# Routing two sequences of a top-2 mixture of experts in one pass, with one-hot tables built on ScalarE

## The chip, the cores and the metric

One NeuronCore of one Trainium2 chip runs the kernel. The metric is the device time of one execution in microseconds (us). PE is TensorE, DVE is VectorE, ACT is ScalarE, POOL is GpSimd; SP issues most of the transfers. Sequences, chunks, blocks and experts are counted from 0.

## The reference

Four sequences of 768 tokens go through linear attention with decay, with 8 heads of width 64; the 3072 rows of width 512 then go through a mixture of 8 experts, two for each token.

```python
for t in range(S):                      # attention, each batch and head
    state = gamma * state + outer(k[t], v[t])
    y[t] = scale * q[t] @ state
x = y as rows of tokens                 # [3072, 512]
noisy = x @ w_gate + log1p(exp(x @ w_noise)) * noise
top2, weights = the two largest of noisy, softmax over the two
out[token] += weight * (relu(x[token] @ w1[e]) @ w2[e])   # for both experts e of a token
```

## The kernel before

**The chunk loop.** The tokens are worked in 24 chunks of 128, six to a sequence, by a loop over j whose order is written out by hand. Iteration j gives PE, in this order: `qk(j+1)` (scores of the next chunk, into two PSUM buffers `pA`), `x_turn(j-1)` (attention rows turned to token rows, with the router's logits and the sums of squares, into `pT`, of which there is one), `y_state(j)` (not in a sequence's first chunk), what stands in the list `middle`, then `y_mm(j)` (output into `pY`, and the state update except in a sequence's last chunk). DVE masks the scores (`am`, two products of 128x512), reduces the logits, makes the row scale, and writes the low half of `x_split` after ACT has written the high half; a store to `xbuf` in DRAM follows on SP's queue. ACT empties `pY` (`yt`), the state (`U`) and squares (`sq`). POOL multiplies queries and values by decay tables (`q_scale`, `v_scale`). SP's queue issues the loads of chunk j+4.

Between these stand small steps put in place by iteration: the list `mid` is issued ahead of `x_split(j-1)`, `todo` behind it, `first_todo` (`at0`) behind `sq(j)`. They are the routing of each finished sequence, the half parts of expert 0's weights (`w_lo_half`, 16 instructions of 128x512 on DVE), and the zeroing of the output (`zero_out`, SP).

**Routing.** For each sequence b: `route_x` (softplus, ACT), `route_b` (noisy logits), `route_t` and `route_i` (max and index, one instruction pair for each chunk), `route_m` (one-hots of the two experts), `route_p` (counts on PE), `route_n`, `route_g`, `route_d` (gates, positions), `rest_a`, `rest_r` (slot numbers of the other experts). `own_a` to `own_t` then build, for expert 0, a 128x768 one-hot `a0` of each token's lane and a table `bb0`; `own_m` multiplies them on PE into the slot list of expert 0, `slots` turns it into row numbers. Sequences 0 and 1 fill the first three blocks of expert 0 (384 slots), whose rows are fetched by an indirect DMA on POOL's queue (`gather`) and turned by a DMA transpose on SP's queue (`x_t`). In the loop the three gathers stand in iterations 19, 20, 20 and the transposes in 20, 21, 21.

**Behind the loop.** `early(n)` issues n units of expert 0's first 384 columns: eight `mm1` units (12 matmuls of 384 columns, then `hh` on ACT and `hl` on DVE), three `mm2` blocks. The first unit stands ahead of `x_turn` of chunk 23. Between units come the routing of sequence 3, its own tables, `rest_b` for each sequence, and `rest(n)`: for each of 8 pairs (sequence, choice) two one-hots and a table on DVE (`rest_c`, `rest_d`) and six matmuls (`rest_e`), which give the slots of experts 1 to 7. Experts 1 to 7 follow, each with its gathers, `mm1` columns and `mm2` blocks; a loop for overfull experts ends the kernel.

Of the kernel before, what the change touches and what calls it, by code (L numbers as in the profile page):

```python
# [20 lines left out]
C = 128  # L21
# [76 lines left out]
def moe_kernel(ctx, tc, qT, kT, kt, vt, noise, wgn, w1, w2, ctab, qtab, xbuf, out):  # L98
# [236 lines left out]
    def y_mm(j):  # L335
# [15 lines left out]
        SQ[j] = loads.tile([128, KT, C], BF, name="sq", bufs=2)  # L351
        nc.scalar.activation(SQ[j].rearrange("p n c -> p (n c)"), y, AF.Square)

    def x_turn(j):
# [12 lines left out]
        if c == 0:  # L367
            LG[b] = work.tile([128, NC, 2 * E], F32, name="lg")
# [56 lines left out]
    def route_m(b):

        ny, m8, i8 = R[b]
        oh = work.tile([128, 2, NC, NL], F32, name="oh")
        s4 = [128, 2, NC, NL]
        nc.vector.tensor_tensor(oh, K("lidx")[:, None, None, :].to_broadcast(s4),  # L430
                                i8[:, :, 0:2].rearrange("p c k -> p k c")[:, :, :, None].to_broadcast(s4), op=OP.is_equal)
# [4 lines left out]
        R[b] = (oh, mb, den)
        R["mb", b] = mb

    def route_c(b):

        oh, mb, den = R[b]
        nc.scalar.activation(den, den, AF.Exp)

    def route_p(b):
        mb = R.pop(("mb", b))
        nc.tensor.matmul(POS[:, :NC, :], trib, mb, start=True, stop=True, skip_group_check=True)
        for c in range(NC):
            n = NC - c
            nc.tensor.matmul(POS[:, c + 1:, :], oneb, mb[:, c:c + 1, :].to_broadcast([128, n, NL]),
                             start=False, stop=True, skip_group_check=True)  # L450
# [708 lines left out]
```

## Time and profile before

| | |
|---|---|
| median of 3 runs | 680.64 us (679.03 to 682.36) |
| profiled execution | 680.02 us, span 678.2 us |
| granted clock of TensorE, mean | 0.989 |
| busy over the span | PE 96%, DVE 46%, ACT 43%, POOL 30% |
| chain that ended last | PE 73%, DVE 10%, DMA 7%, issue 6% |

The span runs from the first to the last instruction of the core; the rest of the execution's time lies around it. Shares over the whole span hide the stages: the chunk loop lasts until about 124 us, the experts from there on. A busy PE is not PE at its peak, since matmuls are pipelined; a granted clock of 1.00 is 2.4 GHz, 0.50 is 1.2 GHz.

### The profile page before, as it was taken

The numbers are of one execution on the slowest core, as the hardware profiler recorded it, in microseconds if no ns is written. First come the engines' busy times: TensorE is split into PE (matmuls) and PEld (weight loads), VectorE is DVE, ScalarE is ACT, GpSimd is POOL, SyncE is SP. The second block draws the span as 40 slices with busy tenths as digits, with TensorE's granted clock in tenths as the row PEclk, the third lists the DMA queues.
The fourth block names the chain that finished last, engine by engine and source line by source line (L and its number), as shares of the span: only waits on it lengthen the run. The fifth ranks groups of instructions, "written<-read, shape, count | busy, mean of one in ns | idle before, by whom it ended". The sixth has DMA issues, their size and how long they took to land.

```text
span 678.2 us, 13086 instructions
## 1 busy us (share of the span) xinstructions
PE 648.3 (96%) x5325; PEld 404.5 (60%) x5325; DVE 308.9 (46%) x790; ACT 294.5 (43%) x521; POOL 200.3 (30%) x158
## 2 busy tenths in 40 slices
PE   7998989999999999999999999999999999999991
PEld 5987878657768745554555455545554565456440
DVE  4699999699877321532053205320622162225100
ACT  4785544412645533543354335434543454434110
POOL 3456355033054034203420342044204410430021
PEclk9999999999999999999999999999999999999996
DMA  9999778949487747644764487547645664660132
GB/s 336 393 381 374 258 249 253 343 136 196 152 157 114 267 77 132 200 140 78 134 191 140 82 125 194 140 78 139 180 140 94 124 199 114 120 125 5 16 47 32
DMA packets 90718, 112.87 MB, mean 166 GB/s; under 512 B 57216, under 2 KB 57472, under 8 KB 87072
## 3 DMA queue, kind: packets, MB, share of 16 engines
q1 hardware_dynamic: 78736, 84.95, 41.0%
q0 software_dynamic: 11344, 26.22, 21.6%
q10 hardware_dynamic: 576, 0.84, 0.4%
q8 instruction: 43, 0.70, 0.4%
q14 instruction: 19, 0.16, 0.1%
HBM read 72.67 MB, written 26.21 MB: 146 GB/s over the span
## 4 chain that ended last, share of the span: by engine, by line
PE 73%; DVE 10%; DMA 7%; issue 6%; ACT 1%; POOL 1%; SPq 0%; POOLq 0%; ACTq 0%
PE pH L834 11%; PE pH L836 11%; PE pH L835 11%; PE pO L866 10%; PE pO L868 10%; PE pO L867 10%; DMA out<-ot,idx 4%; PE pT L365 3%; PE pA L317 2%; PE pY L339 2%; DVE am L320 2%; DVE x L390 1%; DMA xe<-xg 1%; PE pY L332 1%; DVE bb L600 1%
## 5 line engine op out<-in xcount | busy, mean ns | idle before, releaser
L855 POOL DMA_INDIRECT out<-ot,idx x54 | 89.9, 1666 | 342.1 <-ACT ot L850 209.3
L834 PE MATMUL pH<-xe,w1h 128*128 128x384 f16 (+5 forms) x576 | 180.8, 314 | 1.8 <-DMA xe<-xg 1.3
L836 PE MATMUL pH<-xe,w1l 128*128 128x384 f16 (+5 forms) x576 | 180.9, 314 | 0.0
L835 PE MATMUL pH<-xe,w1h 128*128 128x384 f16 (+5 forms) x576 | 180.8, 314 | 0.0
L838 DVE SCALAR_TENSOR_TENSOR hl<-pH,hh 128x384 f16<-128x384 f32 (+5 forms) x144 | 75.4, 527 | 190.8 <-ACT hh L837 190.6
L868 PE MATMUL pO<-w2h,hl 128*128 128x512 f16 x384 | 145.5, 379 | 0.0
L867 PE MATMUL pO<-w2l,hh 128*128 128x512 f16 x384 | 145.5, 379 | 0.0
L866 PE MATMUL pO<-w2h,hh 128*128 128x512 f16 x384 | 145.5, 379 | 0.0
L837 ACT ACTIVATE hh<-pH 128x384 f16<-128x384 f32 (+5 forms) x144 | 67.1, 467 | 134.5 <-PE pH L836 132.5
L850 ACT ACTIVATE ot<-pO,gse 128x512 f32<-128x512 f32 (+4 forms) x54 | 37.1, 687 | 171.0 <-PE pO L868 166.5
L206 DVE SCALAR_TENSOR_TENSOR w1l<-wst,wsc,w1h 128x1024 f16<-128x1024 f32 x28 | 35.8, 1284 | 105.9 <-ACT w1h L201 105.9
L713 POOL DMA_INDIRECT xg<-xbuf,idx x54 | 56.1, 1039 | 75.6 <-DVE wacc L621 30.4
L834 PEld LDWEIGHTS <-w1h 128*128 128x128 f16 x576 | 56.9, 99 | 31.3 <-issue 1.5
L836 PEld LDWEIGHTS <-w1l 128*128 128x128 f16 x576 | 56.3, 98 | 30.9
L835 PEld LDWEIGHTS <-w1h 128*128 128x128 f16 x576 | 56.3, 98 | 30.7 <-issue 0.9
L184 ACT ACTIVATE junk<-wst 128x1024 bf16<-128x1024 f32 x64 | 67.2, 1050 | 0.4 <-DMA wst<-w 0.2
L868 PEld LDWEIGHTS <-hl 128*128 128x128 f16 x384 | 37.6, 98 | 45.3
L866 PEld LDWEIGHTS <-hh 128*128 128x128 f16 x384 | 38.1, 99 | 43.9
L867 PEld LDWEIGHTS <-hh 128*128 128x128 f16 x384 | 37.5, 98 | 44.0
L297 POOL TENSOR_TENSOR qs<-in_q,gq 128x512 f32<-128x512 f32 x23 | 29.3, 1275 | 49.3 <-PE pY L332 18.2
L365 PE MATMUL pT<-turn,yt 128*128 128x144 f32 x192 | 30.6, 304 | 6.5 <-DVE x L390 4.4
L201 ACT ACTIVATE w2h<-wst,wsc 128x1024 f16<-128x1024 f32 x32 | 36.5, 1140 | 0.2 <-DVE wsc L162 0.2
(170 smaller groups left out, 684.0 us busy)
## 6 DMA issues: line engine op xcount, KB each, us to landing
wst<-w SPq DMA_DIRECT2D x28, 1024.0 KB, 7.6
in_q<-qT SPq DMA_DIRECT2D x24, 256.0 KB, 5.1
in_k<-kT SPq DMA_DIRECT2D x24, 256.0 KB, 5.2
in_v<-vt SPq DMA_DIRECT2D x24, 256.0 KB, 5.1
in_kt<-kt SPq DMA_DIRECT2D x24, 256.0 KB, 5.2
xbuf<-x SPq DMA_DIRECT2D x24, 256.0 KB, 5.1
out<-zero SPq DMA_DIRECT2D x6, 1024.0 KB, 8.4
wst<-w SPq DMA_DIRECT2D x8, 512.0 KB, 6.5
```

The costliest lines, as they stand in the source:

```text
L184: nc.scalar.activation(junk, st[:, i * 1024:(i + 1) * 1024], AF.Square, accum_out=ss[:, i:i + 1])
L365: nc.tensor.matmul(p[:, s, g * 128:g * 128 + XW], y[:, s, g, :], turn[:, v, 2 * s + g], start=(g == 0), stop=True, skip_group_check=True)
L713: nc.gpsimd.indirect_dma_start(out=x[:n], out_offset=None, in_=xbuf[:128 + B0 * S] if e == 0 and t < 3 else xbuf, in_offset=bass.IndirectO ...
L834: nc.tensor.matmul(p[:, :n], whi, xh, start=(k == 0), stop=False)
L835: nc.tensor.matmul(p[:, :n], whi, xl, start=False, stop=False)
L836: nc.tensor.matmul(p[:, :n], wlo, xh, start=False, stop=(k == KT - 1))
L837: nc.scalar.activation(hh[:, f, n0:n1], p[:, :n], AF.Relu)
L838: nc.vector.scalar_tensor_tensor(hl[:, f, n0:n1], p[:, :n], 0.0, hh[:, f, n0:n1], op0=OP.max, op1=OP.subtract)
L855: nc.gpsimd.indirect_dma_start(out=out, out_offset=bass.IndirectOffsetOnAxis(ap=idx[:n, i:i + 1], axis=0), in_=ot[:n], in_offset=None, com ...
L866: nc.tensor.matmul(p, a, WT["2h"][:, f, :], start=(f == 0), stop=False)
L867: nc.tensor.matmul(p, a, WT["2l"][:, f, :], start=False, stop=False)
L868: nc.tensor.matmul(p, c, WT["2h"][:, f, :], start=False, stop=(f == FT - 1))
```

## The change

Sequences 0 and 1 form group 0 (12 chunks), sequences 2 and 3 are groups 1 and 2; `SPAN` gives first chunk and count. The routing steps of group 0 run once over 12 chunks, except `route_x`, `route_b`, max and index, which run on six chunks each in iterations 6 to 8 and 12 to 14. `rest_a`, `rest_r` and `rest_b` leave the loop and run once over all 24 chunks behind it. The one-hots of group 0, and those of the `rest` pairs of sequences 0 and 1, are made by ACT as relu(1 - (lane - number)^2): one Square for each chunk, with the negative lane number as bias, and one Relu over six chunks. The gathers move to iterations 20, 21, 21, the transposes to 21, 22, 22. `own_a`, `own_h`, `own_b` of sequence 2 and half part 4 of w2 go behind the loop; half parts of the weights get other iterations; `sq` has one buffer. `rest_e` lags two parts instead of one. The core of the diff:

```diff
+    sfa = consts.tile([128, 2, NCH], F32, name="sfa")
+    ga = consts.tile([128, 2, NCH], F32, name="ga")
+    nla = consts.tile([128, 2, NCH], F32, name="nla")
+    lfa = consts.tile([128, 2, 2, NCH], BF, name="lfa")
...
+    POS = {n: pR[:, :(n + 1) * NL].rearrange("p (c e) -> p c e", c=n + 1) for n in (NC, 2 * NC)}
+    LST = [pR[:, 160:160 + NV * NBLK].rearrange("p (v n) -> p v n", v=NV) for g in range(1)]
     SUM = pR[:, 480:488]
+
+    SPAN = {0: (0, 2 * NC), 1: (2 * NC, NC), 2: (3 * NC, NC)}
+
+    def temp(shape, dt, name, n):
+        pool = RP[0] if n == NCH else work
+        return pool.tile(shape, dt, name=f"{name}_{n}", **({} if n == NC else dict(bufs=1)))
...
-        SQ[j] = loads.tile([128, KT, C], BF, name="sq", bufs=2)
+        SQ[j] = loads.tile([128, KT, C], BF, name="sq", bufs=1)
...
+    def route_b(g, c0, c1):
+
+        b0, n = SPAN[g]
...
+            R[g] = temp([128, n, NL], F32, "ny", n), temp([128, n, 8], F32, "m8", n), temp([128, n, 8], U32, "i8", n)
+        ny = R[g][0][:, c0:c1]
+        nc.vector.tensor_tensor(sp[:, c0:c1], sp[:, c0:c1], nz[:, b0 + c0:b0 + c1, :], op=OP.mult)
         nc.vector.memset(ny[:, :, 0:1] if o else ny[:, :, E:NL], -3.0e38)
-        nc.vector.tensor_tensor(ny[:, :, o:o + E], sp, lg[:, :, :E], op=OP.add)
-        m8 = work.tile([128, NC, 8], F32, name="m8")
-        R[b] = (ny, m8, work.tile([128, NC, 8], U32, name="i8"))
...
+    def own_a(g):
...
         nc.vector.tensor_scalar(lb[:, 1], si, 7, None, op0=OP.arith_shift_right)
-        lf = work.tile([128, 2, NC], BF, name="lf0")
+        lf = temp([128, 2, n], BF, "lf0", n)
         nc.vector.tensor_copy(lf, lb)
-        R["own", b] = lf
-
-    def own_h(b):
-        lf = R["own", b]
-        a = work.tile([128, NC, 128], BF, name="a0", bufs=2)
-        nc.vector.tensor_tensor(a, lanes[:, None, :].to_broadcast([128, NC, 128]),
-                                lf[:, 0, :, None].to_broadcast([128, NC, 128]), op=OP.is_equal)
-        R["own", b] = (lf, a)
+        if g == 0:
+            R["nl", g] = nl = temp([128, n], F32, "nl0", n)
+            nc.vector.tensor_scalar(nl, lb[:, 0], -1.0, None, op0=OP.mult)
+        R["own", g] = lf, temp([128, n, 128], BF, "a0", n)
+
+    def one_hot(a, nl):
+
+        n = nl.shape[-1]
+        for c in range(n):
+            nc.scalar.activation(a[:, c], lanes, AF.Square, bias=nl[:, c:c + 1])
+        nc.scalar.activation(a, a, AF.Relu, bias=1.0, scale=-1.0)
+
+    def own_h(g, c0, c1):
+        lf, a = R["own", g]
+        s3 = [128, c1 - c0, 128]
+        if g == 0:
+            one_hot(a[:, c0:c1], R["nl", g][:, c0:c1])
+            return
+        nc.vector.tensor_tensor(a[:, c0:c1], lanes[:, None, :].to_broadcast(s3),
+                                lf[:, 0, c0:c1, None].to_broadcast(s3), op=OP.is_equal)
 
...
+    def rest_a():
+
+        s3 = [128, NCH, NL]
+        ov = temp(s3, F32, "ov", NCH)
+        sl = temp(s3, F32, "sl", NCH)
+        nc.vector.tensor_scalar(ov, posb, float(CAP), BIG, op0=OP.is_ge, op1=OP.mult)
+        nc.vector.tensor_tensor(sl, posb, K("base")[:, None, :].to_broadcast(s3), op=OP.add)
+        nc.vector.tensor_tensor(ov, ov, sl, op=OP.add)
+        t = temp([128, 2, NCH, NL], F32, "t", NCH)
+        nc.vector.tensor_tensor(t, oh, ov[:, None].to_broadcast([128, 2, NCH, NL]), op=OP.mult)
+        nc.vector.tensor_reduce(sfa, t, axis=AX.X, op=OP.add)
+
+    def rest_b():
+
+        si = temp([128, 2, NCH], I32, "si", NCH)
+        nc.vector.tensor_copy(si, sfa)
+        lb = temp([128, 2, 2, NCH], I32, "lb", NCH)
         nc.vector.tensor_scalar(lb[:, 0], si, 127, None, op0=OP.bitwise_and)
         nc.vector.tensor_scalar(lb[:, 1], si, 7, None, op0=OP.arith_shift_right)
-        nc.vector.tensor_copy(lfa[:, b], lb)
-        gate_parts([vvb[:, b, :, :, v] for v in range(NV)], ga[:, b], [2, NC])
+        nc.vector.tensor_copy(lfa, lb)
+        nc.vector.tensor_scalar(nla, lb[:, 0], -1.0, None, op0=OP.mult)
+        gate_parts([vvb[:, :, :, v] for v in range(NV)], ga, [2, NCH])
 
...
-        nc.vector.tensor_tensor(a, lanes[:, None, :].to_broadcast([128, NC, 128]),
-                                lf[:, 0, k, :, None].to_broadcast([128, NC, 128]), op=OP.is_equal)
+        if b < B0:
+            one_hot(a, nla[:, k, b * NC:(b + 1) * NC])
+        else:
+            nc.vector.tensor_tensor(a, lanes[:, None, :].to_broadcast([128, NC, 128]),
+                                    lf[:, 0, k, :, None].to_broadcast([128, NC, 128]), op=OP.is_equal)
...
 
-    for b in range(B - 1):
-        j = (b + 1) * NC
-        r = [(f, (b,)) for f in (route_b, route_m, route_n, route_g, route_d, rest_a, rest_r, own_a, own_h, own_b, own_t)]
-        at0(j, route_x, b)
-        put_steps(j + 1, [r[0]], [(route_t, (b, 0)), (route_t, (b, 1)), (route_i, (b, 0))])
-        put_steps(j + 2, [(route_i, (b, 1))], [r[1]])
-        at0(j + 2, route_c, b)
-        middle.setdefault(j + 3, []).append((route_p, b))
-        put_steps(j + 3, [r[2]], [r[3], r[4]])
-        put_steps(j + 4, [r[5]], [r[6], r[7]])
-        put_steps(j + 5, [r[8]], [r[9]])
-        if b < B - 2:
-            put_steps(j + 6, [r[10]])
-            middle.setdefault(j + 7, []).append((own_c if b == 0 else own_m, b))
-        if b == 1:
-            put_steps(j + 7, [(own_s, (b,)), (slots, (0, 3))])
-            for t in range(3):
-                at(j + 7 + (t > 0), gather, 0, t)
-                at(j + 8 + (t > 0), x_t, 0, t)
+    mid = {}
...
+    def P(j, f, *a, d=mid):
+        d.setdefault(j, []).append((f, a))
+
+    for j, c in ((6, 0), (12, 6)):
+        at0(j, route_x, 0, c, c + 6)
+        P(j + 1, route_b, 0, c, c + 6)
+        P(j + 1, route_t, 0, c, c + 3)
+        at(j + 1, route_t, 0, c + 3, c + 6)
+        P(j + 2, route_i, 0, c, c + 3)
+        at(j + 2, route_i, 0, c + 3, c + 6)
+    P(15, route_m, 0)
+    at0(15, route_c, 0)
+    P(16, route_p, 0, d=middle)
+    P(16, route_n, 0)
+    at(16, route_g, 0)
+    P(17, route_d, 0)
+    at(17, own_a, 0)
+    at0(17, own_h, 0, 0, 6)
+    at0(18, own_h, 0, 6, 12)
+    at(18, own_b, 0)
+    at(19, own_t, 0)
+    P(20, own_m, 0, d=middle)
+    P(20, own_s, 0)
+    P(20, slots, 0, 3)
+    for t in range(3):
+        at(20 + (t > 0), gather, 0, t)
+        at(21 + (t > 0), x_t, 0, t)
+    at0(18, route_x, 1, 0, 6)
+    at(20, route_b, 1, 0, 6)
+    P(21, route_t, 1, 0, 3)
+    at(21, route_t, 1, 3, 6)
+    at(21, route_i, 1, 0, 3)
+    P(22, route_i, 1, 3, 6)
+    at(22, route_m, 1)
+    at0(22, route_c, 1)
+    P(23, route_p, 1, d=middle)
+    P(23, route_n, 1)
+    at(23, route_g, 1)
+    at(23, route_d, 1)
     at(0, turn_table, 0)
     at(3, turn_table, 1)
     for i in range(4):
...
-    for w, d in (("1", ((mid, 6), (todo, 6), (mid, 8), (todo, 8), (todo, 10), (todo, 11), (todo, 12), (todo, 14))),
-                 ("2", ((todo, 14), (todo, 16), (todo, 17), (mid, 18), (todo, 18)))):
+    for w, d in (("1", ((mid, 6), (todo, 6), (mid, 9), (todo, 9), (mid, 10), (todo, 10), (mid, 11), (todo, 11))),
+                 ("2", ((todo, 15),) + ((mid, 17), (mid, 18), (mid, 19),))):
         for i, (d, j) in enumerate(d):
             d.setdefault(j, []).append((w_lo_half, (0, w, i)))
     at(2, nc.vector.tensor_copy, lanes, K("lanes"))
...
     def rest(n):
-        while done:
+        while len(done) > (1 if n else 0):
             rest_e(*done.pop(0))
         for _ in range(n):
             if parts:
...
     x_turn(j)
-    own_t(b - 1)
     logits(j)
-    route_x(b)
...
+    route_b(2, 0, NC)
     MM[1] = True
-    for i in range(2):
-        route_t(b, i)
-    for i in range(2):
-        route_i(b, i)
-    route_m(b)
-    route_c(b)
+    route_t(2, 0, NC)
+    route_i(2, 0, NC)
+    route_m(2)
+    route_c(2)
+    own_a(1)
+    own_h(1, 0, NC)
     early(2)
-    route_p(b)
-    route_n(b)
-    own_c(b - 1)
-    route_g(b)
+    own_b(1)
+    own_t(1)
+    route_p(2)
+    route_n(2)
+    route_g(2)
     early(1)
-    route_d(b)
-    own_a(b)
-    own_h(b)
+    route_d(2)
+    own_a(2)
+    own_h(2, 0, NC)
     early(1)
-    own_b(b)
-    own_t(b)
-    w_lo_half(0, "2", 5)
+    own_c(1)
+    own_b(2)
+    own_t(2)
+    for i in [4, 5, 6, 7][:2]:
+        w_lo_half(0, "2", i)
     early(1)
-    w_lo_half(0, "2", 6)
-    w_lo_half(0, "2", 7)
+    for i in [4, 5, 6, 7][2:]:
+        w_lo_half(0, "2", i)
     early(1)
     out_scale(0, 0, 3)
 
...
     hook.append(third)
     early(1)
-    rest_a(b)
-    rest_r(b)
-    rest_b(0)
+    rest_a()
+    rest_b()
     rest(1)
+    early(1)
     ranks()
-    rest_b(1)
     for r in range(E - 1):
...
     w_load(1, "2", 0, 2)
     w_load(1, "2", 2, 2)
     out_scale(0, 3, NBLK)
-    early(1)
-    rest(2)
+    rest(1)
     early(len(units))
+    rest(1)
     for t in range(3):
...
                     w_sum(1, "12"[(n - 7) // 4], (n - 7) % 4)
                 if more and e and len(cols) * FT - 5 <= n < len(cols) * FT - 1:
                     w_sum(e + 1, "1", n - (len(cols) * FT - 5))
-                if e == 0 and n in (1, 8):
-                    rest_b(b - 1 if n == 1 else b)
-                if e == 0 and n in (0, 3, 6, 10, 13):
+                if e == 0 and n in (1, 4, 7, 10, 13):
                     rest(1)
                 n += 1
         if more and e:
...
```

## Rows read from the trace of the kernel before

**Rows 1.** Busy time in stretches of 25 us: engines, granted clock, DMA share, GB/s.
```profile
50.00:75.00 25.00, 21.81 (x333) 19.55 (x333) 24.01 (x68) 13.58 (x27) 12.47 (x11) 0.93 0.92 338
75.00:100.00 25.00, 21.64 (x353) 19.27 (x351) 23.86 (x82) 12.70 (x23) 13.34 (x12) 1.00 0.76 249
...
125.00:150.00 25.00, 24.45 (x160) 13.99 (x158) 19.29 (x92) 5.99 (x14) 3.09 (x4) 1.00 0.65 235
...
225.00:250.00 25.00, 25.00 (x147) 14.16 (x146) 6.85 (x14) 10.65 (x19) 4.54 (x4) 1.00 0.45 131
```

**Rows 2.** The same for the chunk loop: PE, weight load, DVE, ACT, POOL.
```profile
12.91:124.05 111.14, 102.30 (x1661) 91.98 (x1658) 97.98 (x331) 66.20 (x130) 53.66 (x46) 0.98 0.91 319
```

**Rows 3.** Waits of PE in the chunk loop: us in total, times, longest.
```profile
PE pT L365 <- DVE x L390: 4.4, 5, 1.5
PE pA L317 <- issue: 1.9, 2, 1.2
PE pT L365 <- DVE cb L475: 1.4, 2, 0.8
PE pT L365 <- DVE m L418: 0.7, 2, 0.5
```

**Rows 4.** Timeline of PE: qk of four iterations, first matmul of expert 0.
```profile
21.77 1.16 PE L317 MATMUL pA<-qs,in_k 64*128 64x128 f32 x16
...
26.21 1.16 PE L317 MATMUL pA<-qs,in_k 64*128 64x128 f32 x16
...
95.58 1.70 PE L317 MATMUL pA<-qs,in_k 64*128 64x128 f32 x16 [1.20 <-issue]
...
124.05 0.34 PE L834 MATMUL pH<-xe,w1h 128*128 128x384 f16 x1
```

**Rows 5.** PE busy time and granted clock in stretches of 1 us.
```profile
65.00:66.00 1.00, 0.05 (x1) 0.96 0.70 268
66.00:67.00 1.00, 1.00 (x4) 0.50 0.50 180
...
69.00:70.00 1.00, 1.00 (x24) 0.83 0.84 219
```

**Rows 6.** Timelines of DVE and POOL: masking products, route_b's product, POOL's product.
```profile
40.29 1.28 DVE L320 TENSOR_TENSOR am<-pA,ct 128x512 f32<-128x512 f32 x2
...
41.85 1.12 DVE L408 TENSOR_TENSOR sp<-sp,nz 128x48 f32<-128x48 f32 x1
...
106.27 0.20 DVE L408 TENSOR_TENSOR sp<-sp,nz 128x48 f32<-128x48 f32 x1
...
41.62 1.28 POOL L297 TENSOR_TENSOR qs<-in_q,gq 128x512 f32<-128x512 f32 x1 [1.85 <-DMA in_q<-qT]
```

**Rows 7.** Groups of instructions by shape: count, busy us, mean ns, idle before.
```profile
L184 ACT ACTIVATE junk<-wst 128x1024 bf16<-128x1024 f32 x64 | 67.2, 1050 | 0.4 <-DMA wst<-w 0.2
...
L390 DVE SCALAR_TENSOR_TENSOR x<-pT,xsa,x 128x512 f16<-128x512 f32 x24 | 17.8, 743 | 7.4 <-ACT x L389 7.2
L389 ACT ACTIVATE x<-pT,xsa 128x512 f16<-128x512 f32 x24 | 16.4, 684 | 40.1 <-issue 10.8 <-DVE xsa L383 9.5 <-PE pY L332 8.4
...
L592 DVE TENSOR_TENSOR a<-lanes,lfa 128x768 bf16<-128x768 bf16 x8 | 7.6, 950 | 0.0
...
L303 ACT ACTIVATE gq<-gq,ct 128x128 f32<-128x128 f32 x20 | 6.2, 391 | 4.6 <-DMA ct<-ctab 4.6
```

**Rows 8.** Timeline of SP's queue near the loop's end.
```profile
117.24 3.81 SPq L720 DMA_TRANSPOSE xe<-xg  x2
```

**Rows 9.** DMA issues of the same stretch, us from issue to landing.
```profile
xe<-xg SPq DMA_TRANSPOSE x2, 3.8
```

**Rows 10.** Timeline of DVE behind the loop: the last half weight parts.
```profile
142.26 1.41 DVE L213 SCALAR_TENSOR_TENSOR w2l<-wst,wsc,w2h 128x512 f16<-128x512 f32 x2
```

**Rows 11.** The chain that ended last: mm2 of block 0.
```profile
142.11 0.22 PE pO L866
```

More of the change, by code (lines that the diff above doesn't have):

```diff
@@ L418, in route_t, with route_i, span @@
+    def route_t(g, c0, c1):
+        ny, m8, i8 = R[g]
+        for c in range(c0, c1):
             nc.vector.max(m8[:, c, :], ny[:, c, :])
-    def route_i(b, n):
-        ny, m8, i8 = R[b]
-        for c in range(3 * n, 3 * n + 3):
+    def route_i(g, c0, c1):
+        ny, m8, i8 = R[g]
+        for c in range(c0, c1):
             nc.vector.max_index(i8[:, c, :], m8[:, c, :], ny[:, c, :])
[L425 to L430, printed above, removed]
+    def span(g):
+        return slice(SPAN[g][0], SPAN[g][0] + SPAN[g][1])
@@ L435, in route_m @@
         nc.vector.tensor_tensor(den, m8[:, :, 1], m8[:, :, 0], op=OP.subtract)
[L436 to L449, printed above, removed]
+        R[g] = (mb, den)
@@ L450, in route_p, with route_c, route_n @@
+    def route_c(g):
+        nc.scalar.activation(R[g][1], R[g][1], AF.Exp)
+    def route_p(g):
+        mb, n = R[g][0], SPAN[g][1]
+        nc.tensor.matmul(POS[n][:, :n, :], trib, mb, start=True, stop=True, skip_group_check=True)
+        for c in range(n):
+            nc.tensor.matmul(POS[n][:, c + 1:, :], oneb, mb[:, c:c + 1, :].to_broadcast([128, n - c, NL]),
                              start=False, stop=True, skip_group_check=True)
-    def route_n(b):
-        oh, mb, den = R[b]
-        sl = slice(b * NC, (b + 1) * NC)
+    def route_n(g):
+        sl, n = span(g), SPAN[g][1]
+        mb, den = R[g]
@@ L520, in gate_parts, with own_b @@
         nc.vector.tensor_tensor(dst[4], r, dst[3], op=OP.subtract)
-    def own_b(b):
-        l = E if b >= B0 else 0
-        sl = slice(b * NC, (b + 1) * NC)
-        gate_parts([tokb[:, None, sl, v] for v in range(NV)], gateb[:, None, sl, l], [1, NC])
-    def own_t(b):
-        sl = slice(b * NC, (b + 1) * NC)
-        lf, a = R["own", b]
-        ob = work.tile([128, NC, NBLK], BF, name="ob0")
-        s3 = [128, NC, NBLK]
+    def own_b(g):
+        l, n = E if g else 0, SPAN[g][1]
+        sl = span(g)
+        gate_parts([tokb[:, None, sl, v] for v in range(NV)], gateb[:, None, sl, l], [1, n])
@@ new lines, in own_t, with own_c, own_m, own_s @@
+        s4 = [128, n, NV, NBLK]
+        nc.vector.tensor_tensor(bb, ob[:, :, None, :].to_broadcast(s4), tokb[:, span(g), :, None].to_broadcast(s4), op=OP.mult)
+        R["own", g] = (a, bb)
+    def own_c(g):
+        own_m(g)
+        own_s(g)
+    def own_m(g):
+        a, bb = R.pop(("own", g))
+        n = SPAN[g][1]
+        for c in range(n):
+            nc.tensor.matmul(LST[g], a[:, c, :], bb[:, c], start=(c == 0), stop=(c == n - 1), skip_group_check=True)
+    def own_s(g):
+        if g == 0:
+            nc.vector.tensor_copy(acc, LST[g])
+        else:
+            nc.vector.tensor_tensor(acc, acc, LST[g], op=OP.add)
@@ L921, in moe_kernel @@
     x_turn(j)
-    own_t(b - 1)
     logits(j)
-    route_x(b)
+    route_x(2, 0, NC)
     x_scale(j)
```

167 lines of the change are left out of this document (69 added, 98 removed).

## The prediction

> **What bounds the kernel now.** I began with busy time by stretch [rows 1]. From 225 us on TensorE (PE) is busy in all of 25.00 us, and in 125 to 150 us in 24.45; the change can only gain in the first 125 us. There PE has 21.6 to 21.8 of 25 us between 50 and 100, and VectorE (DVE) has 23.9 to 24.0: it is the fullest engine beside PE. One stretch over the chunk loop, from its first regular iteration to the first matmul of expert 0 [rows 2], says it in one line: 111.14 us, PE 102.30, DVE 97.98, ScalarE (ACT) 66.20, GpSimd (POOL) 53.66. PE's waits there [rows 3] are nearly all for DVE: 4.4 us x_turn for x_split, 1.4 and 0.7 us x_turn with another DVE instruction named, and 1.9 us put down to issue, at matmuls of qk whose buffer the masking product on DVE empties. The reader should see that an undisturbed iteration lasts 26.21 - 21.77 = 4.44 us, and that a qk on a half empty buffer is stretched, 1.70 instead of 1.16 us [rows 4].
>
> Second cost of the same waits: after PE had been idle twice between 62 and 66 us, the granted clock went from 1.00 to 0.50 (2.4 to 1.2 GHz) at about 65.96 and came back at about 69.2 [rows 5]; 3.2 us at half rate cost 1.6 us.
>
> So the ceiling is 111.14 - 102.30 = 8.8 us of idle time, 1.6 us of clock and 1.1 us in two stretched qk: 11.5 us. The loop without any of it takes 102.30 - 1.6 - 1.1 = 99.6 us; with the clock loss alone taken off, 100.7. I take 100.1, which ends the loop at 12.91 + 100.1 = 113.0 instead of 124.05. The matmuls for tables and ranks don't change this: 33 in the loop before (three times 7, twice 6), 32 after (13, 12 and 7).
>
> **The change part by part.**
>
> *DVE's routing work.* In an undisturbed iteration DVE owes 1.28 us for two masking products, about 0.3 for logits and scales, and 0.7 for its half of x_split [rows 6, 7], which leaves some 2.2 us. Before, iterations 9 to 11 and 15 to 18 mostly held a routing stage, an own or rest stage and one or two half weight parts of 0.7 us. After, 12 chunks are routed with the instruction count of 6 in all stages but max and index; rest_a, rest_r and three 128x768 one-hots (0.95 us each when free [rows 7]) leave the loop, and one half weight part. Going through the new order by iteration, extra DVE work is at most about 1.6 us everywhere except 7 and 13. I therefore cost the removed waits fully, by the loop's 100.1 us. Bounds: 0 removed (124.05 stays) and everything removed (112.5).
>
> *What stays: route_b.* Its product took 1.12 us at 41.85 and ended as POOL's product (41.62 + 1.28) did; with POOL idle it took 0.20 [rows 6]. That is a wait for POOL, and it isn't touched. The two route_b of the joint group still stand ahead of x_split, and now three max instructions (about 0.25 us) stand between them too. Before, this wait cost PE 0.7 us [rows 3]; I put 0.7 + 2 x 0.25 = 1.2 us back. Bounds 0.7 and 2.
>
> *One-hots on ACT.* Six chunks are six Squares and one Relu. The nearest row for a Square is the 128x128 scale with a per-partition operand, 6.2 us for 20, 0.31 each back to back; for the Relu over 768 the bounds are a 128x512 (0.68) and a 128x1024 (1.05) [rows 7]; I take 0.85. So 6 x 0.31 + 0.85 = 2.7 us, twice, behind sq of iterations 17 and 18. Queued behind them on ACT are x_split's first half, then yt; behind those, x_turn on PE. With T the start of iteration 17: own_a's last result is there at T + 6.1 (x_split of chunk 16 ends at 4.8, then five instructions of 0.17 and 0.5 behind POOL's product), the first half runs to T + 8.9, x_split of chunk 17 ends on DVE at T + 10.2 (two halves of 0.7); but x_turn of chunk 18 could start at T + 8.9 (iterations 17 and 18 last 4.0 and 3.8, without state update and y_state, then qk 1.1): PE waits about 1.4 us. The second half ends at about T + 14.0 with route_x(1); it costs a further 0.6. Then DVE's delay in 22 holds x_turn of chunk 22 some 0.3 us. I take 2.3 us; bounds 0 (both halves fall into ACT's gaps) and 5.4 (both wholly on PE's path).
>
> The Trainium skill speaks against this step: "ScalarE: Activation LUTs", section "Rules for kernel authors", would leave multiplications and maxima to VectorE because it is faster per element. The trace agrees on the price, 0.95 us on DVE against my 2.7 on ACT. By the rule the sum would be about 2 us shorter, if DVE had room in 17 and 18, which its new order gives it; by the rows of before, where DVE is full [rows 1], it hadn't. This is an argument of its own, and the numbers here go by the rows.
>
> *Slot tables one iteration later.* The gathers move from iterations 19 and 20 to 20 and 21, and the transposes of blocks 1 and 2 from 21 to 22. On SP's queue these stand behind the store of chunk 21, which waits for x_split of iteration 22. Before, the two transposes were issued from 117.24 to 121.05 [rows 8], with 3.8 us from the start of an issue to landing [rows 9]: the last landed near 119.15 + 3.8 = 122.95, and the first matmul, which reads all three blocks, started at 124.05 without a wait [rows 4]: 1.1 us to spare. After, x_split in 22 ends about 4.2 us into it: 2.8 until the scales are there (an estimate: qk 1.16 [rows 4], x_turn about as long, the scales), then 0.68 and 0.74 for its two halves [rows 7]; or 5.0 with DVE's max_index work in front; the transposes are issued from 4.6 to 5.4, the second 1.9 later, landing at 10.3 to 11.1. Iterations 22 and 23 leave PE 4.44 and about 3.2 us of work (no qk, no state update in 23), 7.7 together, 8.2 with the wait above. So PE stands still for 2.1 to 3.4 us before expert 0; I take 2.7. Nothing covers this: x_turn of chunk 23 is queued behind those matmuls. POOL's queue is passed too: the gathers stand behind two products each and land earlier than SP gets to the transposes.
>
> *The clock in that wait.* An idle stretch of 2.7 us in one piece is longer than either that preceded the fall at 66 us. If it falls again, up to 1.6 us is lost [rows 5], less what of the low time lies in the wait itself. Between 0 and 1.6 I take 0.9.
>
> *Behind the loop.* own_a, own_h, own_b of sequence 2 and one more half weight part (0.7 [rows 10]) come into a stretch that had DVE busy for 19.3 of 25 us [rows 1]: about 3 us more. The last half of w2l was ready at 143.7; mm2 of block 0 begins at 142.1 [rows 10, 11] and comes to that half after 23 of 24 matmuls of 0.22 us, at about 147, so a delay of 3 us just fits. Blocks 3 to 6 are gathered as much later, which may show. On ACT one one-hot in the second set of mm1 columns holds hh for 2.7 us, and three buffers turn meanwhile. I take 0.6 us for all three; bounds 0 and 2. rest_a and rest_b over all sequences cost DVE some 2 us each (5 and 9 instructions of 0.2 to 0.5, an estimate) and lie under mm2, which asks DVE for nothing; that cover gone, they would delay the second set's hl. The one buffer for sq and the later table flush cost nothing: x_turn has read sq before the next is written.
>
> **Sum.** 113.0 + 1.2 + 2.3 + 2.7 = 119.2 against 124.05: 4.85 us gained; 0.9 and 0.6 given back: 3.35 us. The profiled execution's time is 680.02 (span 678.2 and 1.8 around it), so 676.7; it lay 0.6 under the median of the three runs, 680.64, on which I forecast 677.2.
>
> **The rivals.** I call 0.5%, 3.4 us, what can be told from no change.
> A. *Full relief.* ACT finishes both halves in its gaps (66 of 111 us busy speaks for it), the clock holds and the last wait is its lower 2.1: 113.0 + 1.2 + 2.1 = 116.3, 7.7 us gained, 673 us. Against it: nl is late in iteration 17 whatever ACT does. Chance 0.25.
> B. *Gained and given back.* The loop ends early, but the wait for the transposes is 4 us, the clock falls for the full 1.6, and the stretch behind the loop costs 2: 113.0 + 1.2 + 2.3 + 4 = 120.5, 3.55 gained, 3.6 lost: 680.7. For it: the transposes and tables are tied to the same few instructions. Chance 0.27.
> C. *Slower: ACT becomes the loop's bound in 17 to 20.* Both one-hot halves come on PE's path wholly (5.4 us) and push the tables by another 4: PE is then idle twice long enough for a clock loss, 3.2 us. 113.0 + 1.2 + 5.4 + 2.7 + 4 = 126.3, plus 3.2 and 1: 6.5 us slower, 687 us. It decides from about 11 us of waits in the loop; before, ACT's 40% idle time speaks against it. Chance 0.10. The rule of the Trainium skill named above points to this side; no row of before shows how far.
> My forecast has 0.38; its own range is 675 to 679, which lies on both sides of the bound of 677.2.
>
> **How the numbers follow.** Faster by over 0.5%: A and a little over half of the forecast, 0.47. Within: the rest of the forecast and B, 0.43. Slower: C, 0.10. The range leaves out the far ends of A and C: 671.8 to 682.5.
>
> **What would show it.** DVE's share between 50 and 100 us falls from 96% to near 80%; iterations 9 to 17 go at 4.4 to 4.6 us; x_turn of chunks 18 and 19 waits on ACT or DVE for 1 to 2 us; PE idles 2 to 3.4 us ahead of the first mm1, released by the transposes; PE is full from 125 us on. The prediction is wrong if that last wait is missing, if the loop ends after 121 or before 116 us, or if PE shows waits of several us behind it.

## The result, and the profile after

The changed kernel takes 684.15 us (median of 5 runs, 683.11 to 686.81) against 680.64 (679.03 to 682.36): ratio 1.0058, 95% interval 1.003 to 1.0086. Forecast were 677.2 us and a range of 671.8 to 682.5. Timed once more (experiment 9), 12 runs beside 17 of the kernel before, it had 680.80 against 681.35 us: ratio 1.0011, interval 0.9982 to 1.004. The ratios in this document are estimated from the single executions, not from the two medians, and leave out two slow ones, of 2950 us in experiment 1 and of 687.6 us of the kernel before beside experiments 9 and 10. So the changed kernel is between no change and 0.6% slower; the forecast gain of 0.5% did not come in either comparison. The profiled execution (686.81 us, span 685.0) is the longest of its five.

Busy time in the stretches of [rows 1], same columns:

```profile
50.00:75.00 25.00, 24.03 (x406) 21.61 (x407) 21.71 (x63) 16.82 (x31) 16.91 (x14) 1.00 1.04 388
75.00:100.00 25.00, 22.39 (x343) 20.17 (x345) 21.38 (x61) 17.36 (x38) 11.32 (x11) 0.94 0.81 269
...
12.91:125.23 112.32, 101.44 (x1656) 91.52 (x1657) 87.63 (x275) 72.83 (x145) 54.39 (x46) 0.98 0.94 328
12.91:119.40 106.49, 101.44 (x1656) 91.49 (x1656) 86.56 (x269) 71.60 (x143) 54.39 (x46) 0.98 0.93 334
```

VectorE's share between 50 and 100 us fell from 96% to 86%, and TensorE works 24.03 us between 50 and 75 where it worked 21.81 [rows 1]: the relief is there. The two last lines are the stretch of [rows 2], cut at the first matmul of expert 0 and at the last matmul ahead of it: the same 101.44 us of PE in both, so that PE stands still from 119.4 to 125.23. The waits of PE in the loop, as in [rows 3]:

```profile
PE pH L880 <- DMA xe<-xg: 5.8, 1, 5.8
PE pT L373 <- DVE x L399: 1.9, 3, 0.8
PE pT L373 <- DVE tokb L538: 1.9, 1, 1.9
PE pA L325 <- POOL qs L305: 0.5, 2, 0.3
PE pT L373 <- DVE s L198: 0.5, 1, 0.5
PE pT L373 <- ACT sq L360: 0.2, 1, 0.2
```

The waits for DVE, those put down to issue in [rows 3] among them, have halved, from 8.4 to 4.3 us, and of the 4.3 the 1.9 named `tokb` are due to ACT, as shown below. One wait of 5.8 us for the transposes, missing before, outweighs what was gained. It is the first thing to read here. The granted clock in stretches of 1 us, as in [rows 5], shows what goes with it:

```profile
97.00:98.00 1.00, 1.00 (x19) 0.90 (x21) 0.98 (x4) 1.00 (x4) 0.00 (x0) 0.50 0.85 217
...
100.00:101.00 1.00, 1.00 (x24) 0.93 (x22) 0.99 (x2) 0.47 (x1) 1.00 (x2) 0.82 0.82 279
...
124.00:125.00 1.00, 0.00 (x0) 0.00 (x0) 0.00 (x0) 0.00 (x0) 0.00 (x0) 0.62 1.35 365
...
126.00:127.00 1.00, 1.00 (x5) 0.44 (x3) 0.00 (x0) 0.00 (x0) 0.00 (x0) 0.50 1.04 404
...
131.00:132.00 1.00, 1.00 (x11) 0.67 (x10) 0.08 (x1) 0.49 (x1) 0.00 (x0) 0.96 1.06 414
```

At 1.2 GHz PE works from 96.9 to 100.35 us, which costs 1.7 us, and from the first mm1 at 125.23 to about 131.1, which costs half of 5.85: 2.9 us. The fall at 66 us of [rows 5] is gone.

The instructions behind both stalls, from the timelines of PE, ACT, DVE, POOL and SP's queue (start, duration), and the transposes' landing, as in [rows 4, 6, 8, 9]:

```profile
91.79 1.86 ACT L522 ACTIVATE a<-lanes,nl 128x128 bf16<-128x128 bf16 x6 [1.37 <-DVE nl L515]
93.68 0.84 ACT L523 ACTIVATE a<-a 128x768 bf16<-128x768 bf16 x1
94.43 0.67 ACT L398 ACTIVATE x<-pT,xsa 128x512 f16<-128x512 f32 x1
...
95.14 0.75 DVE L399 SCALAR_TENSOR_TENSOR x<-pT,xsa,x 128x512 f16<-128x512 f32 x1 [1.18 <-ACT x L398]
...
96.03 1.40 PE L373 MATMUL pT<-turn,yt 128*128 128x144 f32 x8 [1.88 <-DVE tokb L538]
...
106.04 2.96 DVE L420 TENSOR_TENSOR sp<-sp,nz 128x48 f32<-128x48 f32 x1
...
106.64 1.28 POOL L305 TENSOR_TENSOR qs<-in_q,gq 128x512 f32<-128x512 f32 x1
107.88 1.05 POOL L299 TENSOR_TENSOR vp<-in_v,ct 128x512 f32<-128x512 f32 x1
...
110.14 1.51 PE L325 MATMUL pA<-qs,in_k 64*128 64x128 f32 x16
...
114.28 0.88 SPq L273 DMA_DIRECT2D out<-zero  x1
...
116.54 4.88 SPq L740 DMA_TRANSPOSE xe<-xg  x2
...
125.23 0.48 PE L880 MATMUL pH<-xe,w1h 128*128 128x384 f16 x1 [5.83 <-DMA xe<-xg]
...
xe<-xg SPq DMA_TRANSPOSE x2, 6.1
```

The first stall reads from the top: six Squares and the Relu hold ACT for 2.7 us, the high half of x_split starts behind them at 94.43, the low half at 95.14, and PE gets pT back at 96.03; the named releaser `tokb` is only the next DVE instruction. The second reads at the bottom: the two transposes go out from 116.54, need 4.88 us for their issue and land 6.1 us after the start of an issue, where [rows 8, 9] had 3.81 and 3.8.

As a mark behind the loop I use the last matmul for the scales of expert 1's first weights, before and after:

```profile
187.78 0.28 PE L188 MATMUL pR<-wss,onef 128*128 128x4 f32 x2
```

```profile
190.42 0.28 PE L196 MATMUL pR<-wss,onef 128*128 128x4 f32 x2
```

It comes 2.64 us later. From there to the end of the span no line differs, yet it took 490.42 us before and 494.58 after; the runs below bear on what that is worth.

### The profile page after: what moved, and what is told of

Its sections match the earlier page's. It is cut to its first block, busy times and chain, and to the rows that moved or that the text cites. A ratio compares the mean times of both kernels' runs of the same rounds, so it can differ in the third digit from the quotient of the medians.

```text
span 685.0 us, 13047 instructions
## 1 busy us (share of the span) xinstructions
PE 653.1 (95%) x5324; PEld 406.9 (59%) x5324; DVE 294.9 (43%) x712; ACT 310.1 (45%) x562; POOL 199.0 (29%) x158
## 4 chain that ended last, share of the span: by engine, by line
PE 77%; DMA 10%; DVE 6%; issue 2%; SPq 2%; ACT 1%; POOL 1%; POOLq 0%; ACTq 0%
PE pH L880 11%; PE pH L882 11%; PE pH L881 11%; PE pO L912 11%; PE pO L913 11%; PE pO L914 11%; PE pT L373 2%; DMA in_k<-kT 2%; DMA in_kt<-kt 2%; PE pY L347 1%; DMA wst<-w 1%; PE pA L325 1%; DMA xbuf<-zero 1%; DMA in_q<-qT 1%; DMA xe<-xg 1%
## 5 line engine op out<-in xcount | busy, mean ns | idle before, releaser
L901 POOL DMA_INDIRECT out<-ot,idx x54 | 87.8, 1626 | 345.4 <-ACT ot L896 228.5
L209 ACT ACTIVATE w1h<-wst,wsc 128x1024 f16<-128x1024 f32 x32 | 36.0, 1138 | 1.3 <-DVE wsc L170 1.2
```

The costliest lines, as they stand in the source:

```text
L209: nc.scalar.activation(hi, st[:, i * 1024:(i + 1) * 1024], AF.Copy, scale=sc[:, 0:1])
L901: nc.gpsimd.indirect_dma_start(out=out, out_offset=bass.IndirectOffsetOnAxis(ap=idx[:n, i:i + 1], axis=0), in_=ot[:n], in_offset=None, com ...
```

## The experiments

Theory: the relief of VectorE is real, and what takes it back is the slot tables that come one iteration later, by the wait for the transposes and the clock behind it. Rivals: the one-hots on ACT take it back, in the loop or behind it; or the stretch behind the mark became slower. Each ratio is to the kernel before on the same chip; experiments 1 to 4 ran on one chip, 5 to 8 on a second, 9 and 10 on a third.

**1. First one-hots back on VectorE.**

```diff
     def own_h(g, c0, c1):
-        if g == 0:
-            one_hot(a[:, c0:c1], R["nl", g][:, c0:c1])
-            return
```

> The changed kernel, but the lane one-hots of group 0 are made by VectorE again (two products of 128x768), in the same places. Theory A (the wait for the transposes and the clock after it are the loss): little changes in the end, the loop may end 1 to 2 us earlier, the transposes are issued as much earlier, 682 to 683 us. Theory B (ScalarE's one-hots are the loss: the 1.9 us wait of x_turn in iteration 19 and the half clock behind it, 1.6 us): both go, 680 to 681 us, and the granted clock stays at 1.00 between 95 and 101 us.

Ratio 1.0014 (0.9992 to 1.0036), 684.16 against 683.07 us. The rows of PE:

```profile
92.72 1.71 PE L325 MATMUL pA<-qs,in_k 64*128 64x128 f32 x16 [0.50 <-issue]
95.26 2.20 PE L373 MATMUL pT<-turn,yt 128*128 128x144 f32 x8 [0.84 <-DVE tokb L535]
...
124.15 0.48 PE L877 MATMUL pH<-xe,w1h 128*128 128x384 f16 x1 [5.54 <-DMA xe<-xg]
```

The wait of 1.88 us became 0.50 and 0.84, the clock still fell behind it (an x_turn of 1.22 us took 2.20), and the wait for the transposes is nearly whole. ACT's one-hots cost the loop about 1.1 us (125.23 against 124.15; 0.5 against the 124.69 of experiment 9) and are not the cause.

**2. The zeroing transfers behind the transposes.**

```diff
-        at((20, 21, 22, 22, 23)[i], zero_out, i)
+        at((22, 22, 22, 23, 23)[i], zero_out, i)
```

> The changed kernel, with the first two zeroing transfers of 1 MB (iterations 20 and 21) issued behind the three transposes, in iteration 22. Theory A1 (the last transposes landed after 6.1 instead of 3.8 us because a zeroing transfer went ahead of them): the wait before expert 0 falls from 5.8 to about 3.5 us, the time to about 681.5. Rival (a pair of transposes takes that long by itself): the wait stays at 5 to 6 us, the time at 684.

Ratio 0.9965 (0.9949 to 0.998), 680.53 us. SP's queue and PE:

```profile
115.76 2.80 SPq L740 DMA_TRANSPOSE xe<-xg  x2
...
96.35 1.22 PE L373 MATMUL pT<-turn,yt 128*128 128x144 f32 x8 [1.88 <-DVE tokb L538]
97.00:98.00 1.00, 1.00 (x25) 0.96 (x23) 1.00 (x2) 1.00 (x4) 0.00 (x0) 1.00 0.77 277
...
121.72 0.32 PE L880 MATMUL pH<-xe,w1h 128*128 128x384 f16 x1 [3.08 <-DMA xe<-xg]
```

Without a zeroing transfer 2.3 us ahead in the queue each transpose is issued in 1.40 instead of 2.44 us, and the second, issued at 117.16, has landed by 121.72: 4.6 us at most instead of 6.1. The wait falls from 5.83 to 3.08. This is in line with the Trainium skill, "DMA: Bandwidth & Descriptors", section "Queues, rings and completion order", by which each DMA engine takes the descriptors of one issuing engine in ring order; that the order alone sets the time is not shown (experiment 6). The ratio is not all due to the edit: in this profile the clock also held in the loop, behind the same wait of 1.88 us (1.00 from 97 to 98 us, where the changed kernel had 0.50).

**3. The wait filled with matmuls on constants** (they add work that nothing reads).

```diff
+    busy(24)
     early(1)
```

> The changed kernel, with 24 matmuls of 128x512 on a constant tile (about 5.2 us at full clock) ahead of the first matmul of expert 0, so that TensorE is not idle while the transposes are under way. Theory: the half clock from 124.4 to 131.0 us costs about 3 us behind the wait; with it gone, the time is 3 us shorter, 681 us, and the clock stays at 1.00. Rival (the clock costs nothing, since VectorE or transfers limit that stretch): 684 us.

Ratio 0.9988 (0.9973 to 1.0003), 682.14 us.

```profile
120.61 5.13 PE L115 MATMUL pA<-warm 128*128 128x512 bf16 x23 [0.16 <-issue]
125.91 0.32 PE L880 MATMUL pH<-xe,w1h 128*128 128x384 f16 x1 [0.18 <-DMA xe<-xg]
...
126.00:127.00 1.00, 1.00 (x7) 0.59 (x7) 0.00 (x0) 0.00 (x0) 0.00 (x0) 1.00 1.07 416
```

mm1 starts 0.7 us later than in the changed kernel, but at 2.4 GHz, and from mm1 to the mark it takes 62.13 us where the changed kernel took 65.19: the clock behind the wait costs 3.06 us, by the windows 2.9. The gain is read from the trace: the interval of the ratio holds 1, and the changed kernel was not timed on this chip.

**4. The joint group one iteration earlier throughout**, from route_m to the transposes, so that tables, gathers and transposes stand where they stood before.

```diff
-    P(15, route_m, 0)
+    at(14, route_m, 0)
...
-    at0(17, own_h, 0, 0, 6)
-    at0(18, own_h, 0, 6, 12)
+    at0(16, own_h, 0, 0, 6)
+    at0(17, own_h, 0, 6, 12)
...
-        at(20 + (t > 0), gather, 0, t)
-        at(21 + (t > 0), x_t, 0, t)
+        at(19 + (t > 0), gather, 0, t)
+        at(20 + (t > 0), x_t, 0, t)
```

> The changed kernel, with routing and tables of group 0 from route_m on, its gathers and transposes, all one iteration earlier (gathers in 19, 20, 20, transposes in 20, 21, 21, as in the kernel before). Theory A (the transposes' place is the loss): the wait before expert 0 falls from 5.8 to 0 to 1.5 us, the clock holds there, 676 to 678 us. Theory B (ScalarE's one-hots): the waits in the loop move one iteration forward and stay, 683 to 684 us.

Ratio 0.9887 (0.9863 to 0.9912), 675.6 us: faster than both kernels.

```profile
94.13 2.26 PE L373 MATMUL pT<-turn,yt 128*128 128x144 f32 x8 [1.85 <-DVE x L399]
...
121.13 0.34 PE L880 MATMUL pH<-xe,w1h 128*128 128x384 f16 x1
```

No wait ahead of mm1, which starts 4.1 us earlier, and no clock loss behind it (62.14 us to the mark), though the wait for ACT's one-hots and the clock fall behind that are as they were.

**5. The kernel before, profiled again.**

> The kernel before, unchanged, for a second profile. In the profiles of the changed kernel and of the variants so far, 493.5 to 495.8 us pass from the last scaling matmul of expert 1's first weights to the end of the span, against 490.4 in the profile of before, although no line differs there. If this belongs to the single execution, the new profile of before shows it too: 493 or more. Rival: what the change leaves behind (other buffers, other queue order) slows the experts by 3 to 5 us; then the new profile shows 490 to 491 again.

This execution ran at a granted clock of 0.85 nearly throughout (mean 0.845, span 763.3 us) and says nothing on the point.

**6. The kernel before with the delay alone.**

```diff
-                at(j + 7 + (t > 0), gather, 0, t)
-                at(j + 8 + (t > 0), x_t, 0, t)
+                at(j + 8 + (t > 0), gather, 0, t)
+                at(j + 9 + (t > 0), x_t, 0, t)
```

> The kernel before with one edit: the gathers and transposes of the first three blocks one iteration later, as in the change. Theory: the transposes are issued one iteration (some 4.5 us) later, near 121.7, and land 3.8 to 6.1 us after the second issue, so TensorE waits 3.4 to 5.7 us ahead of expert 0 and loses 1.6 to 2.9 us of clock behind it: 4 to 8 us slower than before, ratio 1.006 to 1.012. Rival: the store of chunk 22 and x_turn hide the shift, since the tables were ready early anyway: within 1 us of before.

Ratio 1.0095 (1.0062 to 1.0127), 689.93 against 682.32 us: 7.6 us by the medians, 6.5 by the ratio.

```profile
118.18 0.58 SPq L265 DMA_DIRECT2D out<-zero  x1
...
120.70 3.47 SPq L720 DMA_TRANSPOSE xe<-xg  x2
122.90 1.27 SPq L720 DMA_TRANSPOSE xe<-xg  x1
...
126.24 0.32 PE L834 MATMUL pH<-xe,w1h 128*128 128x384 f16 x1 [2.95 <-DMA xe<-xg]
```

The edit alone makes the wait (2.95 us) and a clock loss behind it. Its profile is of one of the shorter executions (685.37 us), with the mark only 3.85 us late, at 191.63: 2.19 us by the later mm1, 1.66 by the clock behind it. The four executions under 687 us had a mean granted clock of 0.987 to 0.992, the six above 689 of 0.981 to 0.985; 0.006 of 680 us is 4 us, an estimate by which the rest of the 7.6 goes with the clock, but where it fell in those no profile shows. The second transpose, which the last row of the queue shows by itself, was issued at 122.90 and had landed 3.3 us later at most, although a zeroing transfer had gone out 2.5 us ahead of the first.

**7. The rest pairs' one-hots on VectorE** (in rest_c, for sequences 0 and 1).

```diff
-        if b < B0:
-            one_hot(a, nla[:, k, b * NC:(b + 1) * NC])
-        else:
-            nc.vector.tensor_tensor(a, lanes[:, None, :].to_broadcast([128, NC, 128]), ...)
+        nc.vector.tensor_tensor(a, lanes[:, None, :].to_broadcast([128, NC, 128]), ...)
```

> The changed kernel with the one-hots of the rest pairs of sequences 0 and 1 back on VectorE (four times a Square for each of six chunks and a Relu leave ScalarE, four products of 128x768 come to VectorE). In the changed kernel 65.2 us pass from the first mm1 to the last scaling matmul of expert 1's first weights, 62.3 without the clock loss, against 63.7 before. Theory: the 1.4 us gained there come from the steps over all sequences and the wider spacing, not from the engine: the stretch stays within 0.5 us, ratio to before 1.004 to 1.007. Rival 1: the relief of VectorE (4 x 0.95 us) brought them: the stretch is 1 to 2 us longer. Rival 2, as predicted: ScalarE's one-hots hold hh, and the stretch is 0.6 us shorter.

Ratio 1.0009 (0.9982 to 1.0035), under the 1.004 to 1.007 expected. First mm1 at 124.32, the mark here:

```profile
189.30 0.28 PE L196 MATMUL pR<-wss,onef 128*128 128x4 f32 x2
```

That is 64.98 us from mm1 to the mark; PE worked at 1.2 GHz until about 129.6, which is 2.6 us of it, and 62.4 without that. The changed kernel has 62.3, the kernel before 63.73, and the four variants that lost no clock there (3, 4, 8 and 10) 62.13 to 62.16. So the stretch gained some 1.4 to 1.6 us, and the engine of these one-hots matters for none of it; that the steps over all sequences and their new places brought it is what is left, not tested by itself.

**8. Early tables, one-hots in quarters** (three chunks on ACT in 16 and 17, three on DVE in 17 and 18; the diff is to variant 4).

```diff
-    at0(16, own_h, 0, 0, 6)
-    at0(17, own_h, 0, 6, 12)
+    at0(16, own_h, 0, 0, 3)
+    at0(17, own_h, 0, 3, 6)
+    at(17, own_h, 0, 6, 9)
+    at(18, own_h, 0, 9, 12)
...
-        if g == 0:
+        if g == 0 and c0 < 6:
             one_hot(a[:, c0:c1], R["nl", g][:, c0:c1])
```

> The variant with the tables one iteration early, and its first one-hots in quarters: three chunks on ScalarE behind the squares of iterations 16 and 17, three on VectorE in 17 and 18. Theory: half a one-hot (some 1.4 us) fits into ScalarE's gap, x_turn of chunk 17 no longer waits 1.85 us, the clock holds, and 1.6 us of clock come back too: first mm1 near 118, 671.5 to 673.5 us where the variant with halves has 675.6. Rival: the wait moves on, to the next x_turn or to the transposes, which now have 3 us less cover: less than 1 us gained.

Ratio 0.9889 (0.9857 to 0.9922), 674.81 us.

```profile
91.96 1.22 PE L373 MATMUL pT<-turn,yt 128*128 128x144 f32 x8 [0.84 <-DVE x L399]
97.23 1.22 PE L373 MATMUL pT<-turn,yt 128*128 128x144 f32 x8 [0.84 <-DVE x L399]
...
118.99 0.34 PE L882 MATMUL pH<-xe,w1h 128*128 128x384 f16 x1
```

The profile does as the theory said: the wait of 1.85 us became two of 0.84, the clock held behind them (1.00 in each us from 89 to 100), mm1 came at 118.99. The median does not show it: 674.81 us lies above the 671.5 to 673.5 expected, and the ratio is that of variant 4.

**9. The changed kernel again.**

> The changed kernel itself, timed again beside the kernel before. Two variants of it whose edits move no wait by more than 1 us had ratios of 1.0014 and 1.0009. Theory: by the traces (2.6 us more at the last scaling matmul of expert 1's first weights, the same experts behind it) the ratio is 1.002 to 1.005. Rival: the 5 us that the first profile showed behind that matmul belong to the change, and the ratio is 1.006 to 1.010.

Ratio 1.0011, as given above; it lies under the ranges of both theories, next to no change; its interval, up to 1.004, leaves the first open.

```profile
116.70 3.94 SPq L740 DMA_TRANSPOSE xe<-xg  x2
...
118.46 1.09 PE L347 MATMUL pY<-am,vp 128*64 128x128 f32 x16
124.69 0.48 PE L880 MATMUL pH<-xe,w1h 128*128 128x384 f16 x1 [5.14 <-DMA xe<-xg]
...
121.00:122.00 1.00, 0.00 (x0) 0.00 (x0) 0.00 (x0) 0.00 (x0) 0.00 (x0) 0.81 1.04 15
...
128.00:129.00 1.00, 1.00 (x8) 0.83 (x6) 0.00 (x0) 0.00 (x0) 0.00 (x0) 0.78 1.03 371
...
188.65 0.28 PE L196 MATMUL pR<-wss,onef 128*128 128x4 f32 x2
```

The same wait, 5.14 us, and the mark 0.87 us later than before; from the mark to the end of the span 678.7 - 188.65 = 490.05 us. The clock behind the wait, by the rows in stretches of 1 us, cost less than in the first profile: it had fallen at about 121.6, while PE still waited, and was back at about 128.4, so mm1 ran at 1.2 GHz for 3.75 us, which costs 1.9. In the first profile it fell only at 124.2 and was back at 131.1, and mm1 had 5.85 us of it. The same kernel thus pays 1.9 or 2.9 us for much the same wait, by how much of the low clock lies within the wait.

**10. Early tables, one-hots wholly on VectorE** (to variant 8).

```diff
-    at0(16, own_h, 0, 0, 3)
-    at0(17, own_h, 0, 3, 6)
-    at(17, own_h, 0, 6, 9)
-    at(18, own_h, 0, 9, 12)
+    at(16, own_h, 0, 0, 6)
+    at(17, own_h, 0, 6, 12)
...
-        if g == 0 and c0 < 6:
-            one_hot(a[:, c0:c1], R["nl", g][:, c0:c1])
-            return
```

> The variant with the tables one iteration early, its first one-hots wholly on VectorE (two instructions of 128x768 in 16 and 17, nothing on ScalarE). Theory: with its new order VectorE has room for 1.9 us in these two iterations, and the result is that of the quarters, 674 to 675.5 us: the gain of the best version comes from the order and from the early tables, not from the engine. Rival: VectorE is full there, x_split comes later and a wait of over 1 us with a clock fall appears in iterations 17 to 19: 676 to 678 us.

Ratio 0.9886 (0.9851 to 0.9921), 673.01 against 681.35 us, the lowest median of all.

```profile
86.66 1.76 DVE L528 TENSOR_TENSOR a<-lanes,lf 128x768 bf16<-128x768 bf16 x1
...
92.41 0.95 DVE L528 TENSOR_TENSOR a<-lanes,lf 128x768 bf16<-128x768 bf16 x1
...
91.91 2.26 PE L373 MATMUL pT<-turn,yt 128*128 128x144 f32 x8 [1.08 <-ACT sq L360]
...
119.47 0.32 PE L877 MATMUL pH<-xe,w1h 128*128 128x384 f16 x1 [0.35 <-DMA xe<-xg]
```

The first of the two met POOL's product (1.76 us instead of 0.95), the clock was low from about 91 to 97.9 as the rival had it, and still the ratio is that of 4 and 8. Which engine makes the first one-hots is worth less than these runs can tell.

## Why the prediction was wrong

The failed step is the slot tables one iteration later. The mechanism was right, a wait for the transposes and a low clock behind it; its two prices, 2.7 and 0.9 us, were too small by 5.1 us together in the first profile and by 3.4 in the second. Next to it stands the loop: a clock fall that the sum had at nothing, and 1.5 us more of idle time than it had, together 2.9 us after 0.4 less of PE's own work; the stretch behind the loop gave 2.0 back. To the mark the sum was 184.4 (187.78 - 4.85 + 0.9 + 0.6); the two profiles of the changed kernel have 190.42 and 188.65, 6.0 and 4.2 more. By terms:

| term of the sum | forecast | first profile | difference | second profile | difference |
|---|---|---|---|---|---|
| loop's end without the last wait | 116.5 | 119.4 | +2.9 | 119.6 | +3.1 |
| wait for the transposes | 2.7 | 5.8 | +3.1 | 5.1 | +2.4 |
| clock behind that wait | 0.9 | 2.9 | +2.0 | 1.9 | +1.0 |
| behind the loop, without clock | +0.6 | -1.4 | -2.0 | -1.7 | -2.3 |

**Wait for the transposes.** The forecast had the last one land 10.3 to 11.1 us into iteration 22. The iteration begins at 110.14, so the issue came at 6.4 instead of 4.6 to 5.4, the second after another 2.44, and it landed 6.1 later: 15.0. PE reached its end 9.3 into it instead of 7.7 to 8.2. By the timelines, the issue was late because x_split of chunk 20 stood behind route_b's product, which took 2.96 us beside POOL's two instead of the 1.12 of [rows 6]; x_turn of chunk 21 waited 0.84 us for it, and x_split of chunk 21 came after that. The prediction priced this wait for POOL at the joint group's two route_b and not at that of sequence 2 in iteration 20; no run takes it away. Issue and landing were long in part because of the zeroing transfer ahead in SP's queue: the prediction named only the store of chunk 21 ahead of the moved transposes, and took their duration from the old place. Experiment 2 takes the transfer away, and the wait is 2.75 us shorter. How far ahead it was issued does not explain the rest: 3.8 us in the kernel before (113.45, and 117.24 in [rows 8]) with 3.81 us of issue, 3.5 in experiment 4 with 4.62, 2.5 in experiment 6 with 3.47, and 2.3 in the two profiles of the changed kernel with 4.88 and 3.94. What else sets these times stays open. Experiment 4 takes the whole delay away and has no wait; experiment 6 puts the delay alone into the kernel before and makes it slower.

**The clock in that wait.** The bound of 1.6 us was taken from [rows 5] and was no bound: behind the wait the low time was 5.85 us long in the first profile and 3.75 in the second, at a cost of 2.9 and 1.9. That part of the low time can lie in the wait itself the prediction had allowed for, and the two profiles differ in just this. Experiment 3 keeps PE at work and gets 3.06 back. Two small slips of the prediction change nothing: by [rows 5] the low clock at 66 us lasted to 69.3, which costs 1.7 and not 1.6, and the 673 of rival A leaves out the 0.6 behind the loop.

**DVE's routing work.** The relief came, if less in VectorE's share (86% instead of near 80). PE's own work, 101.44 - 1.7 of clock = 99.7 us, is the 100.1 of the forecast. But the loop had 5.0 us of idle time instead of 3.5, the surplus in waits of 0.2 to 0.8 that I had put at nothing, and the clock loss of 1.7 us that I had taken away with the stalls at 66 us came back behind the stall at 96. The loop's gain is then 124.05 - 119.4 = 4.65 us, not 7.55.

**One-hots on ACT.** The price was right to the digit (1.86 + 0.84 = 2.7), and so was the place; the wait was 1.88 instead of 1.4. The second half was priced at 0.6 and shows no wait, but it ran from 96.26 to 99.0, while PE was at 1.2 GHz; in experiment 2, where the clock held, the x_turn behind it waited 0.40. That PE's clock could fall behind it was in rival C only. The rule of "ScalarE: Activation LUTs", section "Rules for kernel authors" in the Trainium skill, which would leave this work to VectorE, is not contradicted: with VectorE relieved, experiments 1 and 10 lose nothing by following it, and no run shows a measurable gain by it.

**Behind the loop** I forecast a loss and there was a gain. The two waits at pB ahead of the rest matmuls, 0.8 us together before, are gone; the last half of w2l was just in time, as forecast, with no wait of PE in mm2. The remainder of the 1.4 us is not traced.

**The time to the end.** From the mark to the end, with the same code, the nine profiles of the experiments other than 5 took 489.8 to 495.8 us, and they sort by the chip: 493.5 to 495.8 in experiments 1 to 4, 492.0 to 492.7 in 6 to 8, 489.8 and 490.05 in 10 and 9. On the second of these chips the kernel that routes as before took 492.0 (experiment 6) and two with the new routing 492.35 and 492.7, so the change costs at most 0.7 us there, and the 4.2 us between the first two profiles are not the change's in the main. What made them is not shown; the first profile of the changed kernel has 2.0 us of waits put down to issue behind the mark, and a granted clock of 0.83 between 540 and 550 us (about 1.7 us lost), and neither the kernel before nor experiment 9 has these. The mark itself, 0.87 and 2.64 us later than in the only usable profile of the kernel before, is what the traces show the change to cost: 0.1 to 0.4%.

Rival B, *gained and given back*, had the mechanism, with 4 us of wait and 1.6 of clock; its 680.7 us fits the second comparison (1.0011 of 680.64 is 681.4) and is 3.4 us under the first.

The whole fits in four ratios, each good to about 0.3%. With the tables in iterations 19 to 21: before 1, routed jointly 0.9887. With the tables one iteration later: before 1.0095, routed jointly 1.0058 or 1.0011. Joint routing is worth 0.4 to 1.1%, the delay costs 1.0% in the old order and 1.3 to 1.7% in the new, and the change contains both. What stays open is how the delay's cost in the old order divides between wait and clock in its longer executions, and what besides the zeroing transfer sets the time of the transposes.

## What to carry to other kernels

A step that is moved later in a queue is priced with the traffic that it will have ahead of it there, not with the duration that it had at the old place; and a wait that the move opens on TensorE is priced with the clock behind it, which here cost 1.9 or 2.9 us on top of 5.1 and 5.8. Where one change relieves an engine and also delays a result, take the two apart: each alone moved the time by about 1%, in opposite directions, and together they looked like nothing.

## What the runs showed of the hardware

- Two DMA transposes in a row on SP's queue, in this one stretch, took 2.80 us to issue with no zeroing transfer just ahead, and 3.47 to 5.68 us with one 1.9 to 3.8 us ahead, without following that distance; they landed 3.8 us after the start of an issue in the kernel before and 6.1 and 5.9 in the changed one.
- The same wait of 1.88 us was followed by a clock of 0.50 in the changed kernel and by 1.00 in experiment 2; two waits of 0.84 in experiment 8 were not followed by a fall.
- One kernel, two profiles: behind waits of 5.8 and 5.1 us the first matmuls ran at 1.2 GHz for 5.85 and 3.75 us.
- A product of 128x48 on VectorE took 2.96 us beside two products on POOL, and one of 128x768 1.76 us beside one, against 0.20 [rows 6] and 0.95 free [rows 7].
